# At most four swapped weight pieces under way at a time, in a segment-recurrent attention kernel on one core

## The chip, the core and the metric

The kernel runs on one core of a Trainium2 chip. The core has five engines that work side by side, each through its own list of instructions in order: TensorE (PE in the profile; its weight loads are listed as PEld), VectorE (DVE), ScalarE (ACT), GpSimd (POOL) and SyncE (SP), which here only issues transfers. Sixteen DMA engines move the data between HBM and the on-chip memory SBUF. Engines tell each other of finished work by semaphores; a transfer raises its semaphore in sixteen steps, and whoever needs the data waits for the last of them.

The metric is the time of one execution on the device in microseconds. The kernel before took 1765.05 us, the median of three runs (1761.03 to 1765.1).

## What is computed

Two branches are mixed by a gate. Branch A runs attention over 64 segments of 32 tokens; each segment also sees 8 memory rows, which the segment before it produced, so the segments follow each other strictly. Branch B is a gated feed-forward network over all 2048 tokens. Cut to what matters:

```python
B, S, Dm = (1, 2048, 640); H, Dh = (32, 192); M, seg = (8, 32)     # branch B: Df = 1536

mem = mem0
for s in range(n_seg):                          # 64 segments
    h = concatenate([mem, xs], axis=1)          # 8 + 32 rows
    q, k, v = (einsum('btd,dhe->bhte', h, W) for W in (Wq, Wk, Wv))
    scores = einsum('bhqe,bhke->bhqk', q, k) * scale
    p = softmax(where(mask, scores, -1e9))
    o = einsum('bhte,hed->btd', einsum('bhqk,bhke->bhqe', p, v), Wo)
    mem = o[:, :M, :]                           # goes into the next segment
    outs.append(o[:, M:, :])
a = concatenate(outs, axis=1)
b = einsum('bsf,fd->bsd', gelu(x @ w_gate) * (x @ w_up), w_down)
g = sigmoid((x * gate_w).sum(-1, keepdims=True))
return g * a + (1 - g) * b
```

## The kernel before

**Stages.** The feed-forward branch comes first, about 200 us, and its result goes to a scratch tensor in HBM (`b_scr`). Then `segment(s)` runs 64 times, some 25 us each. In every segment the attention weights are applied to the segment's rows alone, so that all four matrices are read anew.

**Weights in pieces.** The 32 heads are taken as four octets. Wq, Wk and Wv are cut into pieces `(m, o, k)`: matrix m (0, 1, 2), octet o, and one of five slices k of the 640 input rows; each has 384 KB. Wo is cut into sixteen pieces `(3, p)` of 480 KB. Not all of them fit in SBUF, so 16 places are shared by two pieces each (`partner`, L558 to L561): thirteen pieces of octet 0 (of Wq with k from 2 to 4, of Wk and Wv all five) share theirs with octet 3's, and Wo pieces 0 to 2 with 13 to 15. Even segments go through the octets as 0, 1, 2, 3, odd ones as 3, 2, 1, 0. A segment thus begins with the pieces that the segment before it ended with. When it has used such a piece, it loads the partner into the same place, and needs it late in the same segment. That is a swap: 16 per segment, 6.6 MB.

**Order of work.** `PROG` is the order of a segment, written out by hand: projections by groups (`g`), transposes of q and k (`tq`, `tk`), scores (`sc`), softmax (`ex`), transposes of the probabilities (`pt`), the product with V (`pv`) and the output projection (`wo`). Segments differ by s modulo 4, since the projections of the memory rows of a whole group of four segments ("left" rows, `lf`, `le`, `vb`) are spread over the segments ahead of it. The last output projection, `wo` 3 at L1253, uses the three swapped Wo pieces last. From its result DVE makes the new memory (L1395 and L1399), and the first matmuls of the next segment wait for that.

**Who issues what.** After the feed-forward stage nearly all transfers are issued by SP, in the program's order, and SP waits for each one's conditions before it goes on to the next. After each item of `PROG`, `swap_loads` (called at L1377) issues a swap for each piece that the item has used up, through `load_piece` (L609; the issue itself is L611). Between the swaps in SP's list stand the output store of the segment before (L971) and the load of the next segment's x rows (L719), loads and stores of left rows (L950, L910, L1300), and the loads of the feed-forward result (L962, L967).

**Dependencies.** `_Sched.add` derives an operation's dependencies from the regions that it reads and writes; `finalize` turns them into waits, and `emit_stream` writes them ahead of the operation. A swap depends on the matmuls that read the old piece of its place. Each place has a semaphore of its own, and the matmuls that use the new piece wait for it.

Of the kernel before, what the change touches and what calls it, by code (L numbers as in the profile page):

```python
# [238 lines left out]
def _build(nc, A_x, A_mem0, A_Wq, A_Wk, A_Wv, A_Wo, seg_len, w_gate, w_up, w_down,  # L239
# [34 lines left out]
    S_ = _Sched(nc)  # L274
# [83 lines left out]
    def bview(o, nbytes, plo=0, phi=128):  # L358
        return arena[plo:phi, o // 2:(o + nbytes) // 2]
# [4 lines left out]
    def sreg(o, nbytes, plo=0, phi=128):  # L364
        return Rg("sb", o, o + nbytes, plo, phi)
# [137 lines left out]
    def piece_src(key):  # L503
        if key[0] == 3:
            return Wo2[:, key[1]]
        m, o_, k = key
        return (Wq2, Wk2, Wv2)[m][:, k, OW * o_:OW * (o_ + 1)]

    def piece_size(key):
        return GO if key[0] == 3 else GQ  # L510

    def piece_view(key, o):
        if key[0] == 3:
            return bview(o, GO).rearrange("p (c n) -> p c n", n=Dm)
        return bview(o, GQ)
# [59 lines left out]
    res_off = {}  # L575
# [8 lines left out]
    r_res = {key: sreg(o, piece_size(key)) for key, o in res_off.items()}  # L584
# [13 lines left out]
    slot_id = {}  # L598
# [6 lines left out]
    later = []  # L605

    loaded = {}

    def load_piece(key, name):  # L609
        loaded[slot_id[key]] = key  # L610
        S_.add("sp", lambda e: e.dma_start(piece_view(key, res_off[key]), piece_src(key)), writes=[r_res[key]],  # L611
               dma_sem="slot%d" % slot_id[key], name="%s %s" % (name, key))

    def piece(seg, key):
        order = orders[seg % 2]
# [8 lines left out]
    def swap_loads(seg, item):  # L624
        if item[0] == "g" and item[1] == 0 and 0 < item[2] < KT - 1:
            later.extend(key for key in done_keys if key[0] == 1)
            done_keys[:] = [key for key in done_keys if key[0] != 1]
        elif later:
            done_keys[:] = sorted(done_keys + later, key=lambda key: key[:1] + key[2:])
            del later[:]  # L630
        for key in done_keys:
            other = swap_in.get(key)
            if other is None or (other in partner) == (seg % 2 == 0):
                continue
            load_piece(other, "swap s%d" % seg)
        del done_keys[:]
# [11 lines left out]
    def load_residents(cls, pick=lambda key: True):  # L648
        for key in first:
            if slot_class[key] == cls and pick(key):  # L650
                load_piece(partner[key] if key in tmp_off else key, "res")
# [40 lines left out]
    for h in range(NH):  # L692
        for w_, sb_, rw_, nm in ((w_gate, wg_sb, r_wg, "wg"), (w_up, wu_sb, r_wu, "wu")):
            S_.add("sp", lambda e, h=h, w_=w_, sb_=sb_: e.dma_start(
                sb_[h], w_.rearrange("(p k) f -> p k f", p=128)[:, :, FH * h:FH * (h + 1)]),
                writes=[rw_[h]], dma_sem="%s%d" % (nm, h))
# [230 lines left out]
    for n, (g, o) in enumerate(units):  # L927
# [7 lines left out]
        if g == 0:  # L935
            S_.add("pool", lambda e, o=o, b=b: e.tensor_copy(out=stg[o // 2][:, o % 2], in_=lst[b][:, 0]), reads=[r_lst[b]], writes=[r_stgh[o // 2][o % 2]],
                   name="stg s0 o%d" % o)
# [507 lines left out]
def bass_gated_mix__memory_aug_recurrent_mem_tr__glu_gated_geglu__prompt_kernel(  # L1445
    nc,
    A_x,
    A_mem0,
    A_Wq,
    A_Wk,  # L1450
    A_Wv,
    A_Wo,
    A_seg_len,
    B_x,
    B_w_gate,
    B_w_up,
    B_w_down,
    gate_w,
    out,
):  # L1460
    _build(nc, A_x, A_mem0, A_Wq, A_Wk, A_Wv, A_Wo, A_seg_len, B_w_gate, B_w_up, B_w_down, gate_w, out)
# [33 lines left out]
```

## Time and profile before

| | us |
|---|---|
| median of 3 runs | 1765.05 |
| the profiled execution | 1771.21 |
| its span, first to last instruction | 1769.4 |
| busy: PE / DVE / ACT / POOL | 1606.2 / 959.9 / 803.3 / 400.6 |
| mean granted clock of PE | 0.997 |

The profile's page lists each engine's busy time, the transfers by queue, the chain of work that ended last, the costliest groups of instructions with the idle time before them and what ended it, and each kind of transfer with the median time from issue to landing. Other views show an engine's instructions in order of time, the waits of an engine, that chain in a stretch of time, and for any stretch each engine's busy time, the DMA share (the mean busy share of the sixteen DMA engines) and the rate. "L611" is line 611 of the kernel. SP's waits and issues are not counted as busy time.

### The profile page before, as it was taken

What the parts mean: (1) busy time and instruction counts of PE and PEld (TensorE: products, weight loads), DVE (VectorE), ACT (ScalarE), POOL (GpSimd) and SP (SyncE); (2) the same over time, 40 slices, a digit from 0 to 9 for tenths busy, and PEclk for the clock granted to TensorE, in tenths of its full rate; (3) what the DMA queues carried; (4) which work ended last, traced back from release to release, by engine and by line L of the source; (5) the groups of instructions that cost most, each with busy time, mean ns of one, the idle gap of its engine ahead of it and who ended that gap; (6) DMA issues with size and microseconds to landing.
All of it is one profiled execution on the core that took longest, in us unless ns stands there. A gap on an engine that the chain in (4) does not pass through costs nothing.

```text
span 1769.4 us, 80660 instructions
## 1 busy us (share of the span) xinstructions
PE 1606.2 (91%) x39162; PEld 798.4 (45%) x31501; DVE 959.9 (54%) x2934; ACT 803.3 (45%) x1835; POOL 400.6 (23%) x1358
## 2 busy tenths in 40 slices
PE   9999899989998999889999998988998899989987
PEld 4554444444444444444444444444444444444443
DVE  2222655556565655556555555555565655655554
ACT  3222544545444544445444544444444454444443
POOL 1100222222222222222222222222222222222222
PEclk9999999999999999999999999999999999999999
DMA  9914987888778887878778886878787887879776
GB/s 319 310 45 153 328 314 258 318 306 292 275 271 310 298 312 254 308 289 313 279 273 293 306 314 226 318 283 300 275 284 288 296 315 259 312 276 326 283 277 236
DMA packets 271313, 499.58 MB, mean 282 GB/s; under 512 B 105304, under 2 KB 132208, under 8 KB 270960
## 3 DMA queue, kind: packets, MB, share of 16 engines
q1 hardware_dynamic: 267832, 491.34, 78.2%
q8 instruction: 276, 4.52, 1.0%
q10 hardware_dynamic: 3128, 3.09, 0.5%
q14 instruction: 77, 0.63, 0.1%
HBM read 473.22 MB, written 21.11 MB: 279 GB/s over the span
## 4 chain that ended last, share of the span: by engine, by line
PE 66%; DVE 17%; issue 6%; DMA 5%; ACT 4%; POOL 1%; DVEq 0%; SPq 0%; ACTq 0%; POOLq 0%
PE ps L1061 18%; PE ps L226 14%; PE ps L1230 8%; DMA arena<-in_A_Wo_dram 4%; PE ps L818 3%; PE ps L1201 3%; PE ps L815 3%; PE ps L899 3%; DVE ps L1135 2%; PE ps L1106 2%; DVE arena L1133 2%; PE ps L833 2%; DVE arena L1147 2%; PE ps L1253 2%; DVE arena L1095 2%
## 5 line engine op out<-in xcount | busy, mean ns | idle before, releaser
L1061 PE MATMUL ps<-arena 128*32 128x384 bf16 x9940 | 727.7, 328 | 52.2 <-DVE arena L1399 33.6
L226 PE MATMUL ps<-arena 128*32 128x384 bf16 x7680 | 595.3, 327 | 7.8 <-DVE arena L1239 3.5
L1061 PEld LDWEIGHTS ps<-arena 128*32 128x32 bf16 x9940 | 259.5, 97 | 377.0 <-issue 238.3
L1095 DVE STREAM_TRANSPOSE arena<-arena 128x384 bf16<-128x384 bf16 x512 | 270.6, 557 | 151.3 <-ACT arena L1081 150.3
L1081 ACT ACTIVATE arena<-ps 128x384 bf16<-128x384 f32 x512 | 236.2, 489 | 213.6 <-PE ps L1061 193.2
L1230 PE MATMUL ps<-arena 128*32 128x320 bf16 x6144 | 294.7, 300 | 15.1 <-issue 12.4
L1145 ACT ACTIVATE ps<-ps 104x160 f32<-104x160 f32 x256 | 71.9, 281 | 285.3 <-DVE ps L1135 285.3
L1230 PEld LDWEIGHTS ps<-arena 128*32 128x32 bf16 x6144 | 163.3, 96 | 76.8 <-issue 19.2
L1133 DVE TENSOR_REDUCE arena<-ps 104x4 f32<-104x160 f32 x256 | 82.9, 324 | 163.0 <-PE ps L1121 163.0
L1212 ACT ACTIVATE arena<-ps 128x480 bf16<-128x480 f32 (+1 forms) x256 | 137.0, 535 | 42.5 <-PE ps L1203 37.8
L1098 POOL COPY arena<-arena 64x160 bf16<-64x160 bf16 x256 | 81.3, 318 | 325.3 <-DVE arena L1095 314.2
L1186 ACT ACTIVATE arena<-ps 128x448 bf16<-128x448 f32 x192 | 104.2, 543 | 99.7 <-PE ps L1173 99.1
L1220 POOL COPY arena<-arena 128x96 bf16<-128x96 bf16 x256 | 68.2, 266 | 356.8 <-ACT arena L1212 267.6
L1084 ACT ACTIVATE arena<-ps 128x384 bf16<-128x384 f32 x256 | 125.1, 489 | 26.4 <-PE ps L1061 21.1
L1147 DVE TENSOR_REDUCE arena<-ps 104x4 f32<-104x160 f32 x256 | 83.0, 324 | 93.4 <-ACT ps L1145 93.4
L1201 PE MATMUL ps<-arena 128*64 128x160 bf16 x1536 | 122.1, 242 | 12.1 <-ACT arena L1186 5.8
L1201 PEld LDWEIGHTS ps<-arena 128*64 128x64 bf16 x1536 | 80.8, 109 | 89.1 <-issue 31.6
L899 PE MATMUL ps<-arena 128*32 128x384 bf16 x1280 | 112.7, 332 | 2.4 <-issue 2.4
L956 POOL COPY arena<-arena 128x96 bf16<-128x96 bf16 x256 | 70.3, 275 | 194.1 <-PE ps L1121 130.2
L1203 PE MATMUL ps<-arena 128*64 128x64 bf16 x1536 | 104.8, 194 | 3.9 <-issue 3.9
L1239 DVE TENSOR_TENSOR arena<-ps,arena 64x160 f32<-64x160 f32 x160 | 50.8, 317 | 75.2 <-ACT arena L1236 60.9
L906 DVE STREAM_TRANSPOSE arena<-arena 128x384 bf16<-128x384 bf16 x128 | 73.7, 576 | 31.7 <-ACT arena L904 27.5
(88 smaller groups left out, 2040.7 us busy)
## 6 DMA issues: line engine op xcount, KB each, us to landing
arena<-in_A_Wk_dram SPq DMA_DIRECT2D x335, 384.0 KB, 7.3
arena<-in_A_Wv_dram SPq DMA_DIRECT2D x335, 384.0 KB, 9.1
arena<-in_A_Wo_dram SPq DMA_DIRECT2D x205, 480.0 KB, 6.4
arena<-in_A_Wq_dram SPq DMA_DIRECT2D x209, 384.0 KB, 5.1
arena<-left_qk_scratch SPq DMA_DIRECT2D x126, 96.0 KB, 3.0
left_qk_scratch<-arena SPq DMA_DIRECT2D x49, 192.0 KB, 2.4
left_qk_scratch<-arena SPq DMA_DIRECT2D x30, 96.0 KB, 5.9
ffn_b_scratch<-arena ACTq DMA_DIRECT2D x16, 160.0 KB, 3.8
```

Source lines behind the costliest of these rows:

```text
L226: return e.add_instruction(mybir.InstMatmult(name=nm, start_tensor_calc=like["start"], stop_tensor_calc=stop, tile_size=(128, 32), tile_po ...
L899: fns.append(lambda e, outp=outp, rhs=rhs, j=j: e.matmul(outp, lhs, rhs, start=(k == 0), stop=(k == KT - 1), tile_position=(0, 32 * j)))
L1061: fns.append(lambda e, outp=outp, rhs=rhs, j=j: e.matmul(outp, lhs, rhs, start=(k == 0), stop=(k == KT - 1), tile_position=(0, 32 * j)))
L1081: S_.add("act", lambda e, m=m, bk=bk: e.activation(out=rows_sb[m], in_=ps[:, bk, 0:384], func=ACTF.Copy), reads=[r_ps[bk]], writes=[r_rows ...
L1084: S_.add("act", lambda e, i=i, bk=bk: e.activation(out=v_sb[i % NVB].rearrange("p (c n) -> p c n", c=3), in_=ps[:, bk, 0:384].rearrange("p ...
L1095: S_.add("dve", lambda e: e.transpose(out=dst[:, :, 0:L], in_=rows_sb[m].rearrange("p (c r) -> p c r", r=L)), reads=[r_rows[m]], writes=[r ...
L1133: S_.add("dve", lambda e: e.tensor_reduce(out=mxs, in_=S3, axis=AX.X, op=ALU.max), reads=[rb], writes=[rst], name="smax max")
L1147: S_.add("dve", lambda e: e.tensor_reduce(out=sms, in_=S3, axis=AX.X, op=ALU.add), reads=[rb], writes=[rst], name="smax sum")
L1201: return [lambda e: e.matmul(full, v[:, e0:e0 + 64], PTm[:, i], start=True, stop=False, tile_position=(0, 64 * i), skip_group_check=True), ...
L1203: lambda e: e.matmul(part, vl[:, e0:e0 + 64], PTl[:, i], start=False, stop=True, tile_position=(0, 64 * i), skip_group_check=True)]
L1212: S_.add("act", lambda e: e.activation(out=apx(u[:, 0, 0, :], [[R, na], [3 * R, 4], [1, R]]), in_=ps[:, A, 0:na * W].rearrange("p (c t r) ...
L1230: fns.append(lambda e, i=i, t=t, j=j, gv=gv: e.matmul(ps[32 * j:32 * j + 32, bank, 0:2 * DJ].rearrange("p (h n) -> p h n", h=2), lhs2[i], ...
```

## The change

`load_piece` now remembers the operations that it issues under a name that begins with "swap". From the fifth swap on, each gets one more dependency: on the swap four before it in the order of issue, whose landing SP waits for ahead of the issue. The list runs on over the segments. The loads at the start ("res") are left as they were, as are all other transfers and the order of every list of instructions.

```diff
     loaded = {}
+    NUW = 4
+    under_way = []
 
     def load_piece(key, name):
         loaded[slot_id[key]] = key
-        S_.add("sp", lambda e: e.dma_start(piece_view(key, res_off[key]), piece_src(key)), writes=[r_res[key]],
-               dma_sem="slot%d" % slot_id[key], name="%s %s" % (name, key))
+        op = S_.add("sp", lambda e: e.dma_start(piece_view(key, res_off[key]), piece_src(key)), writes=[r_res[key]],
+                    dma_sem="slot%d" % slot_id[key], name="%s %s" % (name, key))
+        if name.startswith("swap"):
+            under_way.append(op)
+            if len(under_way) > NUW:
+                op.deps.add(under_way.pop(0))
```

## The prediction

> **What bounds the kernel now.** I read the page first, then the SP timeline and chain of waits of one segment, then each transfer's issue and landing, from the updates of its semaphore.
>
> ```profile
> span 1769.4 us, 80660 instructions
> ...
> PE 1606.2 (91%) x39162; PEld 798.4 (45%) x31501; DVE 959.9 (54%) x2934; ACT 803.3 (45%) x1835; POOL 400.6 (23%) x1358
> ...
> q1 hardware_dynamic: 267832, 491.34, 78.2%
> q8 instruction: 276, 4.52, 1.0%
> ...
> arena<-in_A_Wk_dram SPq DMA_DIRECT2D x335, 384.0 KB, 7.3
> arena<-in_A_Wv_dram SPq DMA_DIRECT2D x335, 384.0 KB, 9.1
> arena<-in_A_Wo_dram SPq DMA_DIRECT2D x205, 480.0 KB, 6.4
> ```
>
> TensorE is busy 91% of the span, and the DMA engines 78%, which is no small second place. The pieces take 6 to 9 us to land. Next is the SP timeline of segment 33 (995.0 to 1020.9 us): start, duration, line, number of issues.
>
> ```profile
> 996.77 1.00 SPq L611 DMA_DIRECT2D arena<-in_A_Wk_dram  x1
> 997.82 1.38 SPq L611 DMA_DIRECT2D arena<-in_A_Wq_dram  x3
> 999.23 1.89 SPq L611 DMA_DIRECT2D arena<-in_A_Wk_dram  x4
> 1001.17 2.57 SPq L611 DMA_DIRECT2D arena<-in_A_Wv_dram  x4
> ...
> 1004.94 0.63 SPq L611 DMA_DIRECT2D arena<-in_A_Wv_dram  x1
> 1009.34 0.38 SPq L1300 DMA_DIRECT2D left_qk_scratch<-arena  x1
> 1010.06 0.86 SPq L611 DMA_DIRECT2D arena<-in_A_Wo_dram  x2
> 1010.97 0.43 SPq L1300 DMA_DIRECT2D left_qk_scratch<-arena  x1
> 1011.45 0.74 SPq L611 DMA_DIRECT2D arena<-in_A_Wo_dram  x1
> ```
>
> SP puts twelve pieces into the queue in some 7 us, and they come out one by one: the landings step by 0.97 us for 384 KB and 1.2 us for 480 KB (medians). At its issue a swap of segments 1 to 63 finds up to 9 earlier ones under way; 751 of 1008 find four or more. The chain of waits at the end of this segment, and what the engines did in two stretches of it:
>
> ```profile
> 1011.45 8.22 DMA arena<-in_A_Wo_dram
> 1019.67 0.04 issue
> 1019.72 0.42 PE ps L1253 x12
> 1020.14 0.02 issue
> 1020.16 0.26 DVE arena L1395
> ```
>
> ```profile
> 999.00:1016.00 17.00, 15.02 (x409) 7.91 (x323) 9.96 (x33) 9.01 (x22) 3.13 (x12) 1.00 1.03 379
> 1016.80:1019.60 2.80, 2.15 (x62) 1.05 (x52) 2.02 (x5) 1.79 (x5) 0.46 (x2) 1.00 0.14 52
> ```
>
> The last swapped Wo piece landed at 1019.67, and only then came the last 12 matmuls, the new memory and the next segment. The column before the last, the DMA share, matters most: full until 1016, then 0.14 for the last 2.8 us. The segment waits for a few of the sixteen DMA engines: of the sixteen updates of that piece's semaphore, thirteen had come 6.23 us after the issue, the others at 6.86, 7.17 and 8.22. Sixteen independent queues run in parallel, and the slowest decides.
>
> I took each last Wo piece's slack: from landing to the first TensorE instruction that waits for it. In 62 segments it is under 0.05 us in 19, 0.17 to 0.71 in 10, 0.98 to 2.0 in 16, more in the rest. The 4.6 us that the waits view gives L1253 for these pieces therefore hides how little lies in reserve.
>
> **The change part by part.** It removes, moves and adds no work: the same 1008 swaps run in the same order. It adds to a swap a wait, on SP, for the landing of the swap four before.
>
> *The wait itself.* The first four swaps of a segment find theirs landed (at most three are outstanding). About twelve per segment wait. SP resumes quickly: L950, when it waits for a store's landing, issues 0.017 us after it (15 cases). SP has idle time for one more wait instruction per swap (1012.2 to 1018.6 above); I take 0.
>
> *Can four keep the queue full?* Alone, the first K swap of a segment lands 3.74 us after its issue (62 cases: 3.14 to 5.14; the tenth 3.33, the quarter points 3.55 and 4.25, the ninetieth 4.57). Four pieces in turn take 4 x 0.97 = 3.88 us. A window turns in 3.74 + 0.02 = 3.76, so at the median nothing is lost, with a margin of only 0.12 us. With 4.57 a piece costs (4.59 - 3.88) / 4 = 0.18 us more, over the nine gated pieces to the last V 1.6 us; with 3.33, nothing. The upper half holds cases with small stores and loads just ahead in the queue, so I take 0.1 us at the last V piece and keep 0 to 1.6.
> The Trainium skill, "DMA: Bandwidth & Descriptors", section on the anatomy of one DMA, gives about 2.0 us plus the bytes at 436 GB/s, an estimate of 2.9 us for such a piece. By it four under way leave nearly a microsecond to spare, and this term is 0. The trace has 3.74 and goes first.
>
> *What the depth hides.* Now a delay of one DMA engine holds up only that engine; the others run ahead through up to nine pieces, and a later delay elsewhere vanishes in the maximum. With four, issue follows the slowest engine's landing, the others run dry, and delays of different engines add. The q8 row shows such delays: 276 instruction packets of 16 KB, some 1.02 us each (median of its packets), about four per segment. In segment 33 one ran at 1006.51, and a K piece landed 2.64 us after the piece before it, not 0.97. Another ran at 1012.46, after which two other engines were 0.6 and 0.9 us late while the slowest stayed 2 us late: hidden today, added with a window of four. I take one such packet per segment, 1.0 us at the last Wo piece with the 0.1 above rounded in; the bounds are none and two (0 and 2.0).
>
> *What that costs.* A delay beyond the slack stops TensorE, and L1253, L1395, L1399 and the next segment's first matmuls follow in series, so nothing absorbs it. Over the slacks, a delay of 1.0 us costs 19 x 0.95 = 18 us where the slack is gone, 4.6 us in the ten cases up to 0.71, hardly anything above: 23 us. The same sum gives 9 us at 0.5, 39 at 1.5, 60 at 2.0. K and V pieces: 13 of 611 have under 0.1 us of slack and slip by 0.1 to 0.3 us, but what they stop, Wo gains back: +1.
>
> *What queues behind the waiting swap on SP.* The out store and x load (L971, L719), the L1300 stores, the left loads (L950) and the bz load (L962). They are issued 2 to 6 us later, yet land behind the same pieces as today. The x load landed at 1014.43 and its reader started at 1016.31, released by TensorE (57 of 64 times). The first L1300 store landed at 1016.03, 0.3 us before the V eviction that needs its buffer; its slip runs parallel to that of Wo. The bz load and its left load already follow the second L1300 store's landing. I take 0; without this cover it is the same microsecond, already counted.
>
> **Sum.** 23 + 1 = 24 us. The profiled execution took 1771.2 us (span 1769.4 and 1.8 around it), 6 above the median of 1765.05; 1795 for an execution like it, 1789 for the median. I forecast 1788.
>
> **The rivals.**
>
> *The queue stays full and nothing changes (about 1765 to 1769).* For: the margin of 0.12 us at the median, more at the quarter point of 3.55; if the instruction packets mostly hit the same DMA engine, their sum is already today's maximum. A delay of 0.25 us costs only 4 us. Against: the two engines late after 1012.46 were not the slowest.
>
> *The round trip is longer than the window.* If a swap behind three others takes 4.25 to 4.57 us, each piece costs 0.1 to 0.18 us, and with the packet the last Wo piece comes 1.9 to 2.6 us late: 56 to 89 us, so 1821 to 1854. For: a quarter of the lone first swaps took over 4.25. Against: some of those had other transfers ahead.
>
> *TensorE's instructions arrive sooner: faster.* TensorE's idle time put down to "issue" is 51 us in 72 gaps, and the 50 longest (45 us) end 1.2 to 1.6 us after a q8 packet: it starves for instructions (its 70,663 are 276 x 256). None of the 47 packets with no swap under way was followed by such a gap. With four to nine under way 133 packets cost 31 us, with one to three 84 packets cost 19.5, 0.23 us each in both. If a shallow queue serves these packets as an idle one does, up to 31 us go, and with no loss at Wo about 15 is likely: 1750. It decides if the cost falls with depth between nine and four. Against: per packet it doesn't.
> The Trainium skill, "DMA: Bandwidth & Descriptors", section on queues, rings and completion order, says that each DMA engine takes turns between queues packet by packet; by that the depth of SP's queue would not matter to the instruction queue. The packet times agree: 1.12 us with no swap under way, 0.96 with nine.
>
> **How the numbers follow.** Forecast 0.54, longer round trip 0.15, no change 0.16, faster 0.15. A measurement tells 0.3% (5 us) from no change. Of the forecast 0.53 is slower and 0.01 within; the round trip is all slower; of no change 0.13 is within, 0.02 slower, 0.01 faster; of the last 0.13 is faster, 0.02 within. Slower 0.70, within 0.16, faster 0.14. The likeliest case's own range is 1774 to 1804 (delays of 0.5 to 1.5 us). The whole range, 1755 to 1824, takes in no change, the upper part of the faster case and a delay of 2.0 us.
>
> **What would show it.** SP should wait at L611 mostly for DMA landings, and the medians to landing fall from 7 to 9 us to some 4. If the landings inside a segment still step by 0.97, the queue stayed full; steps near 1.1 mean the round trip. The sixteen updates of the last Wo piece should come closer together while the last comes later against the segment's start. L1253 should wait some 20 us more for Wo pieces. I am wrong if the last landing doesn't move, if another wait takes over (POOL L988 or ACT L1084 for SP's small transfers), or if the "issue" gaps shrink by more than Wo loses.

## The result, and the profile after

The change made the kernel slower: 1829.35 us, the median of four runs (1825.61 to 1839.51), against 1763.9 us for the kernel before in the same comparison (1761.03 to 1765.1). The ratio is 1.038, with a 95% interval from 1.034 to 1.043. So 65 us were lost where 24 were predicted, and the time lies 5 us above the range.

The page of the kernel after, the rows that answer to those of before (line numbers below the change are 6 higher):

```profile
span 1829.7 us, 81183 instructions
...
PE 1630.7 (89%) x39181; PEld 787.8 (43%) x31501; DVE 964.4 (53%) x2934; ACT 803.3 (44%) x1835; POOL 402.4 (22%) x1358
...
q1 hardware_dynamic: 267832, 491.34, 80.1%
...
PE 47%; DMA 30%; DVE 13%; SPq 4%; issue 2%; ACT 2%; POOL 1%; DVEq 0%; POOLq 0%; ACTq 0%
...
L1259 PE MATMUL ps<-arena 128*32 128x160 bf16 x3072 | 85.7, 240 | 57.4 <-DMA arena<-in_A_Wo_dram 47.1
...
arena<-in_A_Wk_dram SPq DMA_DIRECT2D x335, 384.0 KB, 4.8
arena<-in_A_Wv_dram SPq DMA_DIRECT2D x335, 384.0 KB, 4.7
arena<-in_A_Wo_dram SPq DMA_DIRECT2D x205, 480.0 KB, 5.9
```

The last three rows end with the median time from issue to landing: 4.8 and 4.7 us for K and V pieces instead of 7.3 and 9.1. K, V and Wo pieces come sooner after their issue, and the kernel is slower. The row that begins with "PE 47%" says where the time went: it divides the chain of work that ended last, and transfers make up 30% of it now. Before, it read

```profile
PE 66%; DVE 17%; issue 6%; DMA 5%; ACT 4%; POOL 1%; DVEq 0%; SPq 0%; ACTq 0%; POOLq 0%
```

From issue to landing the transfers are not longer. They start later, and so end later in the segment.

SP's timeline of segment 33 of the kernel after (1033.9 to 1061.9 us), with start, duration, line and number of issues:

```profile
1036.08 0.73 SPq L613 DMA_DIRECT2D arena<-in_A_Wk_dram  x1
1036.86 1.57 SPq L613 DMA_DIRECT2D arena<-in_A_Wq_dram  x3
1039.73 5.42 SPq L613 DMA_DIRECT2D arena<-in_A_Wk_dram  x4
1045.40 4.67 SPq L613 DMA_DIRECT2D arena<-in_A_Wv_dram  x4
1050.12 0.59 SPq L977 DMA_DIRECT2D out_dram<-arena  x1
1050.77 0.47 SPq L725 DMA_DIRECT2D arena<-x_scratch  x1
1051.34 0.37 SPq L613 DMA_DIRECT2D arena<-in_A_Wv_dram  x1
...
1052.28 0.98 SPq L613 DMA_DIRECT2D arena<-in_A_Wo_dram  x2
...
1053.90 0.77 SPq L613 DMA_DIRECT2D arena<-in_A_Wo_dram  x1
```

The first twelve pieces took SP 7 us to issue before; now it is 14 (1036.08 to 1050.07), paced by landings. The waits of SP over the whole run (line, what it waited for, us in total, times, longest) name them:

```profile
SPq L613 <- DMA arena<-in_A_Wk_dram: 178.2, 184, 3.6
SPq L613 <- DMA arena<-in_A_Wq_dram: 141.0, 161, 2.3
...
SPq L613 <- DMA arena<-in_A_Wv_dram: 54.1, 82, 1.8
```

The chain of waits at the end of the same segment has the same shape as before:

```profile
1053.90 6.79 DMA arena<-in_A_Wo_dram
...
1060.72 0.42 PE ps L1259 x12
...
1061.17 0.26 DVE arena L1401
...
1061.45 0.26 DVE arena L1405
```

The piece landed 6.79 us after its issue instead of 8.22, but 26.8 us after the start of the segment instead of 24.7 (1060.68 - 1033.9; before 1019.67 - 995.0). Two stretches of that segment, with the DMA share in the column before the last:

```profile
1037.00:1053.00 16.00, 14.72 (x400) 7.24 (x316) 9.69 (x30) 8.81 (x21) 3.53 (x13) 1.00 0.90 300
1057.50:1060.30 2.80, 2.06 (x56) 1.05 (x52) 2.02 (x5) 1.80 (x5) 0.46 (x2) 1.00 0.73 262
```

Before, the main stretch had a share of 1.03 and the last 2.8 us one of 0.14: the engines ran through their queues at full rate, and at the end a few stragglers remained. Now the main stretch has 0.90 (and 300 GB/s in the last column, where it had 379), and the work that was not done there is done at the end, at 0.73. These two rows show the loss in this segment, which grew by 2.1 us. How a late engine costs the others time shows in the sixteen updates of three pieces' semaphores (issue, then us from the issue to each update, sorted):

```
1037.53  3.80 3.83 3.84 3.85 3.88 3.89 3.93 3.95 4.00 4.02 4.05 4.10 4.21 4.73 4.86 5.92
1040.81  3.56 3.58 3.69 3.78 3.89 3.91 3.92 3.99 4.02 4.05 4.11 4.14 4.31 4.42 5.47 5.88
1043.47  2.65 2.67 2.68 2.71 2.73 2.76 2.83 2.83 2.90 3.02 3.18 3.31 3.42 3.43 3.76 4.16
```

One engine was 1.06 us behind the next with the first piece. Its landing, at 1043.46, releases the third, issued at 1043.47, 2.66 us after the swap before it. Thirteen engines had finished the second piece by 1045.12; the first update of the third came only at 1046.12. The thirteenth updates of the second and the third piece lie 1.77 us apart (1045.12 and 1046.89), where 0.97 is usual, so the engines that were on time lost some 0.8 us here, behind the one that was late.

Over all 63 intervals between segment starts, the means are (us):

| | before | after |
|---|---|---|
| start to the first swap's issue | 0.79 | 0.81 |
| that swap to landing | 3.89 | 3.79 |
| first landing to last landing | 17.41 | 19.75 |
| last landing to the next segment | 2.60 | 1.31 |
| sum | 24.71 | 25.66 |

The last landing comes 2.34 us later. Slack takes in 1.29, 0.1 is gained ahead of the first landing, and 0.95 a segment remain: 63 x 0.95 = 60 us, as the spans say (1829.7 - 1769.4). (The 2.60 and 1.31 include some 1.2 us of matmuls and evictions that follow the last landing in any case.)

### The profile page after: what moved, and what is told of

It is laid out like the page before. It is cut to its first block, busy times and chain, and to the rows that moved or that the text cites. A ratio compares the mean times of both kernels' runs of the same rounds, so it can differ in the third digit from the quotient of the medians.

```text
span 1829.7 us, 81183 instructions
## 1 busy us (share of the span) xinstructions
PE 1630.7 (89%) x39181; PEld 787.8 (43%) x31501; DVE 964.4 (53%) x2934; ACT 803.3 (44%) x1835; POOL 402.4 (22%) x1358
## 4 chain that ended last, share of the span: by engine, by line
PE 47%; DMA 30%; DVE 13%; SPq 4%; issue 2%; ACT 2%; POOL 1%; DVEq 0%; POOLq 0%; ACTq 0%
DMA arena<-in_A_Wo_dram 18%; PE ps L1067 14%; PE ps L226 12%; PE ps L1236 5%; DMA arena<-in_A_Wv_dram 4%; DMA arena<-in_A_Wk_dram 4%; DMA arena<-in_A_Wq_dram 3%; DVE ps L1141 2%; DVE arena L1101 2%; PE ps L1112 2%; DVE arena L1139 2%; PE ps L1259 2%; PE ps L839 2%; DVE arena L1153 2%; PE ps L905 2%
## 5 line engine op out<-in xcount | busy, mean ns | idle before, releaser
L1067 PE MATMUL ps<-arena 128*32 128x384 bf16 x9940 | 732.7, 333 | 70.0 <-DMA arena<-in_A_Wv_dram 32.6
L1067 PEld LDWEIGHTS ps<-arena 128*32 128x32 bf16 x9940 | 257.9, 98 | 416.1 <-issue 226.0
L1101 DVE STREAM_TRANSPOSE arena<-arena 128x384 bf16<-128x384 bf16 x512 | 270.9, 558 | 154.4 <-ACT arena L1087 153.8
L1236 PE MATMUL ps<-arena 128*32 128x320 bf16 x6144 | 285.0, 300 | 1.0 <-issue 1.0
L1236 PEld LDWEIGHTS ps<-arena 128*32 128x32 bf16 x6144 | 158.0, 96 | 58.3 <-issue 2.0
L1090 ACT ACTIVATE arena<-ps 128x384 bf16<-128x384 f32 x256 | 125.1, 489 | 53.9 <-PE ps L1067 24.7
L1259 PE MATMUL ps<-arena 128*32 128x160 bf16 x3072 | 85.7, 240 | 57.4 <-DMA arena<-in_A_Wo_dram 47.1
```

The lines of the kernel that those rows point to most:

```text
L1067: fns.append(lambda e, outp=outp, rhs=rhs, j=j: e.matmul(outp, lhs, rhs, start=(k == 0), stop=(k == KT - 1), tile_position=(0, 32 * j)))
L1090: S_.add("act", lambda e, i=i, bk=bk: e.activation(out=v_sb[i % NVB].rearrange("p (c n) -> p c n", c=3), in_=ps[:, bk, 0:384].rearrange("p ...
L1101: S_.add("dve", lambda e: e.transpose(out=dst[:, :, 0:L], in_=rows_sb[m].rearrange("p (c r) -> p c r", r=L)), reads=[r_rows[m]], writes=[r ...
L1236: fns.append(lambda e, i=i, t=t, j=j, gv=gv: e.matmul(ps[32 * j:32 * j + 32, bank, 0:2 * DJ].rearrange("p (h n) -> p h n", h=2), lhs2[i], ...
L1259: S_.add("pe", [lambda e, j=j, c=c, g_=g_, p=p: e.matmul(ps[32 * j:32 * j + 32, OB2, SC:512], u[:, p % 4, c, 0:L], g_[:, c, DJ * j:DJ * (j ...
```

## The experiments

Five theories were tested. A: delays of single DMA engines add up when the others have run dry (the prediction's step). B: four pieces are shorter than the round trip of one. C: a short queue serves TensorE's instruction packets sooner. D: TensorE's instruction gaps shrink only because it waits for weights anyway. E: SP's small transfers, issued between the last V swaps, hold these up.

"Excess" below is how far a segment's fifteen steps between landings exceed 0.97 us (384 KB) or 1.2 us (480 KB), summed. "One late" and "all late" count the steps over 1.3 us among the fifth to eleventh piece of all segments, in us beyond 0.97: one late if the eighth of the sixteen updates had slipped less than half as far as the last, else all late. "Gaps" are TensorE's idle times put down to "issue".

**The depth: five, six, eight, four again, none again.** The edit for five; those for six and eight differ in the number alone:

```diff
-    NUW = 4
+    NUW = 5
```

> Five swaps under way instead of four, nothing else. The profile of the changed kernel has landings 4.5 us per segment over the sum of their usual steps (0.97 and 1.2 us); the kernel before has 2.2. Theory A (delays of single DMA engines add up when the others have no queue left): one piece more in the queue buys 1 us of run-ahead, which hides some of the delays; the excess falls to about 3 us per segment and the time to 1770 to 1800. Rival B (the round trip of a piece is longer than four pieces take): five pieces take 4.85 us, well over the round trip of 3.75, so the excess is at once that of the kernel before (2.2) and the time within 5 us of it.

> Six swaps under way. A: excess about 2.5 us per segment. B: 2.2, as with five. Theory C (TensorE's idle time put down to issue, 51 us before and 5 us after, goes because its instruction packets wait behind a shorter queue): the gaps stay under 25 us although the waits for weights are gone, and the time is 10 to 30 us under the kernel before, 1735 to 1755. Rival D (the gaps go because TensorE waits for weights anyway): the gaps are back near 50 us and the time is 1760 to 1770.

> Eight swaps under way; the kernel before has at most ten. A and B: excess 2.2 us per segment, as before, time 1758 to 1768. C: issue gaps 40 to 50 us, as before. D: the same.

> The changed kernel as it is, as the measure for the other three on the same chip. Both theories: 1.03 to 1.045 times the kernel before; landings 4.3 to 4.7 us per segment over their usual steps, of which about 0.9 at the last V piece and 0.4 to 0.5 at the first Wo piece.

> The kernel before as it is, profiled on the same chip as the other three. All theories: ratio 1.00, landings 2.2 to 2.6 us per segment over their usual steps, TensorE's issue gaps 45 to 55 us.

| depth | ratio, 95% interval | first to last landing | excess | one late | all late | gaps |
|---|---|---|---|---|---|---|
| four (after) | 1.038, 1.034 to 1.043 | 19.75 | 4.51 | 83 | 32 | 5.0 |
| four again | 1.036, 1.030 to 1.042 | 19.85 | 4.61 | 87 | 18 | 6.1 |
| five | 1.017, 1.012 to 1.022 | 18.98 | 3.74 | 52 | 4.5 | 32.6 |
| six | 0.997, 0.994 to 1.000 | 17.81 | 2.57 | 44 | 1.7 | 37.1 |
| eight | 1.000, 0.998 to 1.003 | 17.74 | 2.50 | 47 | 1.9 | 48.1 |
| none (before) | 1 | 17.41 | 2.17 | 49 | 1.1 | 51.4 |
| none again | 0.998, 0.995 to 1.000 | 17.62 | 2.38 | 48 | 0.8 | 41.9 |

The loss sits between four and six, and six is as good as no window at all. B's figure for five (within 5 us of before) is clearly missed: five pieces take 4.85 us to come out, more than the 4.57 us that nine in ten lone swaps need, and yet 30 us are lost (1801.86 against the same kernel before). A's figures for five (an excess of about 3, 1770 to 1800) are missed narrowly. C's figure for six (1735 to 1755) is missed as well: the gaps are 37.1 us, between D's 50 and C's 25, and the time hardly moves. The kernel before, run again, has gaps of 41.9 us and not the 45 to 55 expected, so two executions of one kernel differ by some 10 us there. The row of five also qualifies A: its one-late steps are as before (52 us). Of the 1.4 to 1.6 us that it loses, some 0.8 lie at the last V piece (excess 0.16 to 0.17 without a window, 0.63 with five) and the first Wo piece (0.14 to 0.19, and 0.49).

That the engines run short shows in the packets of the pieces, which take 0.12 us in the median. Without a window 1746 of 129,024 take over 0.4 us, and nearly all stand where the queue has been empty: within 8 us of a segment's first swap, or 14 to 18 us behind it, where the Wo swaps begin. Between 8 and 14 us there are 23. With four there are 3799, of which 1149 stand between 8 and 14 us (3405 and 1102 when repeated), with five 2484 and 479, with six 1729 and 89. With four the time in such packets is 1.1 to 1.5 us more per engine and segment.

**The small transfers.** First without the output store of a segment, so that its rows of the output are not written; then with that store and the load of x issued by ScalarE:

```diff
-                    if s > 0:
-                        out_store(s - 1)
```

```diff
-        S_.add(AUXQ, lambda e: e.dma_start(xs, x_scr[s]
+        S_.add("act", lambda e: e.dma_start(xs, x_scr[s]
...
-        S_.add(AUXQ, lambda e: e.dma_start(out2[L * s:L * s + L, :]
+        S_.add("act", lambda e: e.dma_start(out2[L * s:L * s + L, :]
```

> Four swaps under way, and the store of a segment's 32 rows (40 KB, which runs on four of the sixteen DMA engines, ahead of the last V piece) left out for all segments but the last; so rows of the output are not written. A: the four engines are no longer late, the last V piece's step falls from 1.83 us (mean) to about 1.1, and the time by 35 to 45 us against four with the store, to about 1790. B: only the store's own bytes go, 0.1 us per segment, 6 us in all, to about 1823.

> Four swaps under way; the output store of the segment before and the load of the next segment's x rows are issued by ACT, and no longer by SP behind a swap that waits. Same transfers, same bytes. Theory E (the 1.1 us that SP needs to issue these two after its wait make the next swaps late): the steps at the last V piece and the first Wo piece lose 0.6 to 1.0 us of their 1.3 together, and the time falls by 25 to 50 us against e5. Rival A alone (only late DMA engines count, and the four engines of the store are as late as before): the excess at those two pieces stays within 0.3 us, the time within 12 us of e5.

Measured: 1.028 (1.023 to 1.034) without the store and 1.028 (1.021 to 1.035) with the other issuer, some 14 us better than four again; the intervals overlap, and the executions that were profiled show no gain (1830.94 us with the other issuer, 1831.09 with four again). The last V piece's excess is halved, from 0.86 to 0.43 in the one and 0.32 in the other. But the excess of a segment stays where it was, 4.58 and 4.69, and so does the interval from first to last landing (19.82 and 19.93). E is real at its place: the window opens for the last V swap and SP issues it 0.64 us later (median), since a store and a load stand ahead of it in its list, while the other gated swaps follow in 0.02 to 0.15 us. What is saved there is lost elsewhere: the excess up to the twelfth piece is 3.16 and 3.19, against 2.71 and 2.86 with four. Why is not shown. Both expectations named far larger gains (A 35 to 45 us, E 25 to 50); with the other issuer the last V and the first Wo piece together gained 0.31 us and the time 13 us, about what the rival allowed (0.3 and 12).

**A dose of delay on one engine.** A copy of rows of 1.5 KB from HBM to HBM, all on one DMA engine (in the records its packets follow one another, 65 ns each), once per segment: 17 rows are 1.1 us of that engine, 37 rows 2.4 us.

```diff
+        if name.startswith("swap"):
+            n_swap[0] += 1
+            if n_swap[0] % 16 == 7:
+                S_.add("sp", lambda e: e.dma_start(x17, A_Wq.rearrange("d h e -> d (h e)")[0:17, 0:768]), writes=[Rg("x17", 0, 1)],
+                       dma_sem="x17", watch=True, name="x17")
```

> Four swaps under way, plus one extra copy in HBM per segment behind the seventh swap: 17 rows of 1.5 KB, a number of rows that keeps it on one DMA engine, for about 1 us. It makes one engine late and adds 0.07 us of work to the mean of the sixteen. A (delays add): the last landing of each segment comes 0.7 to 1.1 us later than in e5, 45 to 70 us in all. Rival B (only the round trip of a piece counts): 0 to 0.2 us per segment, under 15 us.

> The same extra copy in the kernel before, whose swaps do not wait for each other. A: the late engine is mostly hidden by another that is late already, and the segment has slack: the last landing 0.2 to 0.5 us later, 5 to 20 us in all, at most a third of what it costs in e7. B: as in e7, under 15 us.

> As e7, with 37 rows in place of 17, which keeps one DMA engine busy for 37 x 65 ns = 2.4 us per segment. A (a late engine stops the issue of further swaps, and the others run dry): the last landing 1.5 to 2.2 us per segment later than with four alone; 85 to 130 us over it, 1.085 to 1.11 of the kernel before. B (only the round trip): 0.15 us per segment for the mean work, under 15 us, at most 1.045.

> The same copy without a window. A: the fifteen others run ahead, the engine joins those that are late by 1.6 us already; the last landing 0.5 to 1.3 us later, of which the slack takes more than half: 5 to 35 us, 1.003 to 1.02. B: under 15 us.

> The same copy with six under way, 2 us of run-ahead. A: between the two, 20 to 60 us over six alone, 1.01 to 1.035. B: under 15 us over six alone (0.997), at most 1.005.

These five expectations speak of a copy behind the seventh swap of a segment. It did not stand there: the count is off by eight, and in the trace the copy follows the fifteenth swap, between the second and third Wo piece of the swapped ones. It could hit only the last piece, with no gated swap of that segment left behind it but one. So the expectations for them can't be judged, and the five runs say nothing of how delays add; they show what a late end costs.

| copy at the end | ratio, 95% interval | first to last landing | mean segment |
|---|---|---|---|
| four, 17 rows | 1.042, 1.037 to 1.048 | 20.31 | 26.09 |
| none, 17 rows | 0.998, 0.996 to 1.001 | 17.74 | 24.63 |
| four, 37 rows | 1.085, 1.081 to 1.090 | 21.36 | 27.08 |
| six, 37 rows | 1.018, 1.013 to 1.022 | 18.96 | 25.31 |
| none, 37 rows | 1.012, 1.009 to 1.015 | 18.61 | 25.07 |

Against the same depth without a copy, the 37 rows move the last landing by 1.5 to 1.6 us with four and by 1.0 to 1.2 without a window, and the segment by 1.4 and 0.4 to 0.5. With four the slack is used up, and nearly every microsecond at the last landing is a microsecond of the segment. Without a window more than half of it is taken in.

**The same dose in the middle.** Now `n_swap[0] % 16 == 15`, which puts the copy of 37 rows between the seventh and eighth swap (so in the trace).

> Window of four, and the copy of 37 rows (some 2.4 us of one DMA engine) now stands right behind the seventh swap of each segment, which it missed in the four runs with a copy before this. A (in a window a late engine stops the issue, the others run dry, and its delay adds to every other one): the step to the eighth or ninth piece grows by over 1.5 us, all sixteen engines carry it on, and first to last landing grows by 1.5 to 2.4 us against 19.75 without the copy; ratio to the kernel before 1.07 to 1.12. Rival (the late engine only joins the maximum at the last landing, as it does with the copy among the Wo pieces): first to last landing grows by no more than in the kernel without a window, ratio under 1.06.

> The kernel before with the same copy behind the seventh swap. A: the other engines run on, the copy's engine is late alone and is taken up in part by delays that are there anyway and by the wait between the V and the Wo pieces: first to last landing grows by 0.4 to 1.2 us against 17.4 to 17.6, ratio 1.002 to 1.02. Rival: grows by as much as with the window of four.

> Window of six with the same copy. A: two more pieces under way (2 x 0.97 = 1.9 us) let the others run on for most of the copy's 2.4 us, so between the two: first to last landing grows by 0.8 to 1.8 us against a window of six alone, ratio 1.005 to 1.04. Rival: as the other two.

(The first of these says four earlier runs; there were five.) "Lag" is how much later the last of the sixteen updates comes than the eighth, in the mean, at the ninth and at the twelfth piece:

| copy in the middle | ratio, 95% interval | first to last landing | growth by the copy | growth of the segment | lag, 9th and 12th piece |
|---|---|---|---|---|---|
| four | 1.066, 1.059 to 1.073 | 20.92 | 1.17 | 1.02 | 1.83, 1.13 |
| six | 1.011, 1.006 to 1.016 | 18.58 | 0.77 | 0.29 | 2.31, 2.20 |
| none | 1.014, 1.010 to 1.018 | 18.70 | 1.1 to 1.3 | 0.4 to 0.5 | 2.42, 2.39 |

TensorE's waits for the last Wo pieces, first with four, then with no window:

```profile
PE ps L1266 <- DMA arena<-in_A_Wo_dram: 58.5, 71, 2.5
```

```profile
PE ps L1260 <- DMA arena<-in_A_Wo_dram: 16.5, 28, 0.9
```

A's figure for four (1.5 to 2.4 us at the last landing) is missed, and the rival's statement holds: a single dose of 2.4 us costs the last landing no more with a window than without. The ratio, 1.066, lies between A's 1.07 and the rival's 1.06. Half of A is seen directly: with four the lag is back at its usual size by the twelfth piece (1.13, and 1.14 without the copy), as when the others are stopped until the late engine has caught up; without a window it stays above the usual (2.39, against 1.77). But while the lag lasts it hides others' delays, with four too: the excess of the ninth to twelfth piece's steps falls from 0.94 us to 0.35 under the dose. So delays that come close together can hide behind each other with a window too. The segment pays more with four (1.02 against about 0.5) because no slack is left, not because the dose grew.

**Without the V and Wo swaps: the gaps alone.** To see TensorE's instruction gaps where no weights are waited for, only the Q and K swaps are loaded, eight per segment. The V and Wo swaps are left out, so an outer octet is computed there with the other one's weights.

```diff
+        if name.startswith("swap") and key[0] > 1:
+            return
```

> Four under way, but only the eight swaps of Wq and Wk in each segment are loaded; the eight of Wv and Wo are left out, so octet 0 or 3 is computed with the other's weights there. TensorE no longer waits for weights. Theory C (a short queue serves TensorE's instruction packets sooner): the issue gaps stay under 12 us. Rival D (the gaps of the changed kernel went only because TensorE waited for weights anyway): the gaps return, 20 us or more, since DMA still runs under about half of the instruction packets.

> The same eight swaps per segment without the window, so up to eight under way in the first part of a segment. C: issue gaps 20 to 40 us, and 10 to 30 us longer than e10. D: the same gaps as e10, and the same time within 8 us.

With four the time is 0.957 of before (0.952 to 0.961), without a window 0.960 (0.956 to 0.964). The spans are 1694.2 and 1701.5 us. One row of the kernel without a window, in its waits of TensorE, has no counterpart in that with four:

```profile
PE ps L1063 <- issue: 6.5, 11, 1.3
```

TensorE waits almost nowhere for weights here (2 us with four), and still the gaps fall from 7.2 us to 0.7. So D, which wanted at least 20 us of gaps with four, falls, although its other figure, times within 8 us, holds (1694.98 and 1702.11 us). C holds in kind: with the shorter queue the instructions come sooner, and the 6.5 us of gaps are most of the 7.3 us between the spans. C's 20 to 40 us without a window do not come.

**A window by segment.** Where there is slack, a short queue should win its gaps for nothing. By s modulo 4, before: last landing to the next segment 3.26, 1.43, 1.80, 4.03 us; gaps 9, 10, 4 and 27 us in all. So four for s modulo 4 = 3, and six, eight and sixteen for the others.

```diff
-    NUW = 4
+    NUW = (6, 8, 16, 4)
...
-            if len(under_way) > NUW:
-                op.deps.add(under_way.pop(0))
+            n = NUW[int(name[6:]) % 4]
+            if len(under_way) > n:
+                op.deps.add(under_way[-1 - n])
```

> The window by the kind of segment (s modulo 4): 6, 8, 16 (more than the ten ever under way) and 4 swaps. Segment lengths by kind in the runs so far: with six 24.33 us for kind 0, with eight 25.05 for kind 1, without a window 23.35 to 23.54 for kind 2, with four 25.01 for kind 3. If they can be put together (A with C): 0.985 to 0.995 of the kernel before, 8 to 25 us less. If the segments with slack only pass their delay on to the next kind, or the gaps return: 0.995 to 1.005.

1762.81 us, ratio 0.996 (0.993 to 0.998), in the second of the two ranges that were expected. The last kind's gaps fall from 27 to 2 us, which is 1.6 us a segment, but its mean segment only from 25.51 to 25.38; in the kernel before, run again, it has 25.33. TensorE's waits show where the rest went (before, 4.6 us at the Wo pieces and 0.2 at the V pieces):

```profile
PE ps L1260 <- DMA arena<-in_A_Wo_dram: 16.7, 25, 1.7
PE ps L1068 <- DMA arena<-in_A_Wv_dram: 7.6, 9, 2.4
```

It has the lowest ratio of the kernels that do the whole work. But the kernel before, run again as an experiment, had 0.998 (0.995 to 1.000): a gain of 0.2 to 0.4% is all that can be claimed.

## Why the prediction was right in sign and too small

**The wait itself: right.** Behind the landing that a swap waits for, SP issues it after 0.02 to 0.15 us (medians by place), but for the last V piece, and 812 of the 1008 swaps find three others under way.

**"What the depth hides": the step that failed.** It took one instruction packet per segment, 1.0 us at the last Wo piece, the 0.1 of the round trip included, with 2.0 as the upper bound. Measured were 2.34 us (2.1 to 2.4 by the repeated runs). The step's mechanism is seen, but it gives only a part of that; the rest comes from terms that the sum had at 0 to 0.1. By place, out of the excess of 2.17 before and 4.51 after: 1.06 us up to the twelfth piece, 0.70 at the last V piece, 0.59 at the three Wo pieces. In the middle, the steps of the fifth to eleventh piece with one engine late grew from 49 to 83 us over the run (87 when repeated). Of these 82 steps, 71 had the end of an instruction packet within them or in the microsecond before, which 36 in 100 of all steps have; that is the step's mechanism, half a microsecond per segment. Not foreseen were the steps in which all engines were late, from 1 us to 18 to 32 over the run, and the end of the segment, where SP issues the last V swap 0.64 us after its window opens. The first of these is also what the rival of the longer round trip would do, but 31 of its 44 steps (24 of the 32 us) had an instruction packet in the same place: whether the queue ran dry by itself or behind a late engine can't be told apart here. Why the three Wo pieces lose 0.59 us was not tried. That delays add one by one is not shown: the dose in the middle grew the last landing by no more than without a window. Together with the lag, which is gone within about four pieces at this depth, this would fit delays that add only when they come far enough apart; no run tests that.

**"Can four keep the queue full": right at the median, not in the mean.** The median steps up to the twelfth piece are still 0.96 to 1.0 us (when repeated, all but the one to the third piece, 1.8). The step to the last V piece takes 1.7 us and that to the first Wo piece 1.5, where 1.1 and 1.2 were usual. The margin of 0.12 us was what the step said, and the upper half of the cases, for which 0.1 us was taken, cost more. The measured time lies in the range of the rival of the longer round trip (1821 to 1854), but not by that rival alone: its sign, steps near 1.1 us throughout, did not come, and with five under way it had nothing left to cost. The 2.9 us from the section on the anatomy of one DMA in the Trainium skill's "DMA: Bandwidth & Descriptors" rest on figures for transfers that GpSimd issues; SP issues the swaps, and the trace had 3.74.

**The price of a delay: right, as far as can be told.** The list by slack (39 us at 1.5, 60 at 2.0) goes on to some 74 at 2.34; 65 came, in which the instruction gaps that went are also counted. By s modulo 4 the means show it:

| s modulo 4 | 0 | 1 | 2 | 3 |
|---|---|---|---|---|
| last landing to next segment, before | 3.26 | 1.43 | 1.80 | 4.03 |
| the same, after | 1.38 | 1.26 | 1.21 | 1.38 |
| growth of first to last landing | 1.86 | 2.34 | 2.39 | 2.73 |
| growth of the segment | 0.14 | 2.44 | 1.37 | -0.29 |

Where there was next to no slack (1), the segment grows by all of the delay. Where there was most (3), it even shrinks, and there 24 of the 46 us of lost gaps were.

**The V pieces: too small.** They were given 1 us; TensorE now waits for them as it does for Wo. Before:

```profile
PE ps L1253 <- DMA arena<-in_A_Wo_dram: 4.6, 11, 0.8
...
PE ps L1061 <- DMA arena<-in_A_Wv_dram: 0.2, 1, 0.2
```

After:

```profile
PE ps L1259 <- DMA arena<-in_A_Wo_dram: 47.1, 61, 2.3
PE ps L1067 <- DMA arena<-in_A_Wv_dram: 32.6, 35, 2.5
```

At the Wo pieces 42 us came where "some 20 more" were forecast. How much of the second Wo gains back was not tried.

**The small transfers: 0 was nearly right for the time.** Moving or dropping them gained some 14 us, if anything, and no other wait took over: ACT waits 8.5 us instead of 0.5 for the stores of left rows (L1090, before L1084), and POOL waits 114 us instead of 44 for the feed-forward rows (L994), but the DVE instruction behind it only 22 instead of 18. That SP's issue time of them delays the last V swap by 0.64 us was not in the sum.

**A sign that did not come.** The sixteen updates of the last Wo piece were to come closer together. In segment 33 they do (2.9 us from first to last before, 1.4 after), but in the mean they don't (2.04 and 2.01).

**The faster rival: right in kind.** The gaps fell from 51 to 5 us, more than the 31 that it claimed, and the argument against it (0.23 us per packet at any depth) fell with that. They even shrank by more than the wait at L1253 grew (46 against 42 us), which the prediction had called a sign of being wrong; the sign was badly chosen, since it left out the V pieces. The gain was 7 us with Q and K swaps alone, where hardly any weights are waited for, and here it was outweighed by the later landings. The Trainium skill, "DMA: Bandwidth & Descriptors", section on queues, rings and completion order, has the DMA engines take turns between queues packet by packet, by which the depth of SP's queue would not matter to instructions; the two kernels with Q and K swaps alone do not bear that out (gaps of 7.2 and 0.7 us).

## What to carry to other kernels

A limit on transfers under way was paid in the mean here, not in the median: a window that just covered the median round trip (3.88 us against 3.76) left nothing for a late engine, and it took two pieces more to lose nothing. Judge it by when the last piece of a stage lands and by the DMA share of the stage, not by the time from issue to landing, which fell from 9 to 5 us while the kernel lost 65. Where a stage has slack after its last landing, a shorter queue need not cost anything; setting the depth by stage was free here, and won little or nothing.

## What was not expected of the hardware

**Instructions and queue depth.** TensorE's instruction gaps went with how much its core had queued for data: 51 and 42 us without a window (two executions), 48 with eight, 37 with six, 33 with five and 5 and 6 with four. Only the last step is clear of the spread, and there TensorE waits for weights as well; the two kernels with Q and K swaps alone show the effect without these waits, at 7.2 and 0.7 us.

**Half clock after short waits.** TensorE's granted clock was 0.50 in 18 stretches of mostly 3.4 us with a window of four (18 again when repeated), in 4 and 2 without one. TensorE's gaps over 0.15 us came to 1.3 to 3.1 us of the 6.8 us ahead of each, and the longest single one was 2.5 us. TensorE's busy time grew by 24 us (1606.2 to 1630.7) for the same work. Little of it seems to lie on the path: the segments that ran at half clock in their first 12 us were longer than others of their kind by 1 us in sum (12 when repeated), and the first swap of a segment is issued 0.81 us after its start in the mean, and 0.79 before. No run here removes the half clock, so its share of the 60 us stays open.
